# A gated FFN beside a long convolution on one core: the conv blocks' loads tied to slots by one-column writes, first kernel rows and FFN leftovers asked for at other places

## The chip, the core and the metric

The kernel runs on one core of a Trainium2 chip. The core has a matrix engine (PE, with its weight loads shown as PEld), a vector engine (DVE), a scalar engine (ACT), a general engine (POOL) and a queue engine (SP), which work side by side and wait for one another by semaphores. Matmul results land in PSUM banks; everything else lives in SBUF. DMA transfers are asked for by an instruction of SP, ACT or POOL, in the order of that engine's own instructions. The metric is the time of one execution in microseconds (us), as the median of several runs.

## What is computed

A layer norm of `x` (2048 positions, 512 channels) feeds two branches. One is a state-space convolution: a kernel `K` of 2048 taps for each channel, made of 128 complex modes, is convolved with the normalised input by FFT, and a skip term is added. The other is a two-layer FFN with a gelu between and a silu behind. The output is `x` plus their product. Cut from the reference:

```python
xn = _layernorm(x)
P = exp((dt * A)[:, :, None] * l)                 # A complex, 512 x 128
K = einsum("dn,dnl,dn->dl", Cc, P, dB).real       # 512 x 2048
s = irfft(rfft(pad(xn.T)) * rfft(pad(K)))[:, :L].T + xn * Dskip
g = silu(gelu(xn @ w1 + b1) @ w2 + b2)            # 512 -> 1792 -> 512
return x + s * g
```

## The kernel before, in words

The work has two parts that follow one another.

**FFN and generation of K.** The first part, up to about 394 us, is played from `ORDER` (line 48), a list of tokens written out by hand; each token calls one function of the table `acts` (line 733), and every engine executes its own instructions in the order in which they were written. The FFN works in 56 steps: four quarters of the positions, twice, with half of the hidden units each time. `F` are the matmuls of the first layer, `G` gelu, `H` and `R` the split of the result into a high and a low part, `S` the matmuls of the second layer (line 277, three matmuls a call, written as `z`). Beside them K is made in 32 pieces; `UD` (line 663) stores a piece from `ko` to the DRAM tensor `kgd`. `KL0` calls `kernel_load(0)`, which loads the first block's kernel rows from `kgd` into `in`; `SL1.g` calls `side_piece(1, g)`, which loads a quarter of block 1's input rows into `raw`. `ZD` stores a gated quarter of the FFN's output to `gd`.

**The last FFN steps.** From line 1071 on the rest is written as a small program. `S0` to `S3` and `L0` to `L3` are the second-layer matmuls of the last two FFN steps. `F00`, `F01`, `F10`, `F11` are the first DFT of conv block 0 (line 864, 64 matmuls of a 32 x 128 weight and 64 columns each; the first digit is 0 for the input and 1 for the kernel rows, the second is the half of the channels), each with its four copies out of PSUM (`first_out`, line 875, two on ACT and two on DVE). A first DFT takes four banks of PSUM. Each `L` is followed on DVE by `z_add`, which adds the first half's sums `zi` (1 MB, loaded by `z_load`, line 398); `A0` to `A3` are silu on ACT. Around these stand the loads of the tables `mc` (line 798, four pieces of 512 KB, the second DFT's cosines and sines) and of `tcn` (`ct_load`, line 806, four pieces of 512 KB, the back DFT's table). `mc_turn` (line 802) makes a negated copy `mn` of a piece on ACT.

**The conv blocks.** Four blocks of 128 channels follow, each of eight slots (`slot`, line 980). Slot `g` of block `b` holds on PE the second DFT of four frequencies (line 882, 64 matmuls, written as `s` like the first DFT), in some slots a back DFT (line 921, written as `sa`) of this block or the one before, in the even slots a first DFT of the next block, and in one slot the last DFT (line 961, written as `y`) of the block before. ACT copies out: `spectrum` (`uh`), the first DFT's outputs (`X`) and the back DFT's (`Z`). DVE multiplies (`product`), combines (`combine`), transposes (`turn`) and, after the last DFT, multiplies by the gate `gb` (`last_out`, line 969), whose sum with `xb` POOL forms. Stores of a finished block go out on SP.

Loads of the blocks, before the change:

- `side_piece` loads four quarters of the input rows of block `b + 2` in slots 3, 4 and 5 of block `b`. One quarter is 256 KB in 128-byte runs. In slot 7 ACT turns `raw` into `in` (`side_turn`, line 837).
- `kernel_load(b + 2)` loads two halves of 512 KB at slot 7; `kernel_load(1)` stands in slot 2 of block 0, on ACT's queue. `side_skip` (line 859) adds the skip coefficient to the rows on POOL.
- `tail_load(b - 1, t)` loads `gb` and `xb` of the block before, quarter by quarter (256 KB each), in slots 0 to 3; the last block's own (`last`) in slots 3 to 6 of the last block.
- `mc` pieces 2 and 3 and `tcn` pieces 1, 2 and 3 are loaded in block 0 on ACT's queue, `mc_turn` 2 and 3 stand in slots 1 and 3.

The tiles named `in` and `raw` share two buffers (tag `in`), so a tile of that tag waits until the readers of the one before the last are through. A load is asked for as soon as its queue has come to it and its tile is free.

Of the kernel before, what the change touches and what calls it, by code (L numbers as in the profile page):

```python
# [11 lines left out]
F32 = mybir.dt.float32  # L12
# [8 lines left out]
P = 128  # L21
L, D, NS, F = 2048, 512, 128, 1792
# [3 lines left out]
N1, N2 = 32, 64  # L26
NB = 4
DB = P // NB
# [4 lines left out]
NQ = L // P  # L33
TB = 4
NTB = NQ // TB
# [86 lines left out]
F.52.1 F.53.0 KL.31.1 UD.26 E.28.1 E.28.2 Z.30 B.30.0 F.53.1 C.30.0 R.51 E.29.0 S.49.2 E.29.1 A.30.1 G.52  # L122
S.49.3 UD.27 Q.28 B.30.1.1 C.30.1 ST S.50.0 SL1.2 H.52 E.29.2 N.30.0 S.50.1 S.50.2 U.28 A.31.0 S.50.3
G.53 S.51.0 F.54.0 B.31.0 C.31.0 A.31.1 Z.31 S.51.1 Q.29 S.51.2 F.54.1 R.52 B.31.1.1 F.55.0 C.31.1 S.51.3
N.30.1 S.52.0 N.31.0 F.55.1 E.30.0 U.29 N.31.1 E.30.1 ZG.2 E.30.2 E.31.0 S.52.1 Q.30 H.53 E.31.1 UD.28
UD.29 S.52.2 R.53 S.52.3 S.53.0 E.31.2 G.54 H.54 U.30 G.55 S.53.1 Q.31 ZD.2 UD.30 H.55 R.54 R.55 U.31
S.53.2 S.53.3 UD.31 KL0
"""


# [37 lines left out]
def kernel(  # L168
# [5 lines left out]
    V, A, GP, PE, SY = nc.vector, nc.scalar, nc.gpsimd, nc.tensor, nc.sync  # L174
# [118 lines left out]
    SB = {}  # L293
# [103 lines left out]

    def z_load(t):
        zi = wka.tile([P, NB, TB, P], F32, tag="zi", name=f"zi{t}")
        (A if t == NTB - 1 else SY).dma_start(zi, za[t])  # L400
        fin[t] = zi

    def bias_load():
# [378 lines left out]
    def open_front():  # L782
        SB["pf"] = pf = opened(p2, "pf", "right")
        SB["mc"] = pf.tile([P, N1, 2, N2], F32, name="mc")
        SB["mn"] = pf.tile([P, N1, N2], F32, name="mn")
        SB["psa"] = opened(p2, "psa", "right", bufs=2, space=PSUM)
# [8 lines left out]
        gx[0] = new_tail(0)  # L795
        yy[0, "T", 1] = new_turn(0, 1)

    def mc_load(j, q=SY):
        k, w = slice(8 * j, 8 * j + 8), 16 * N2
        q.dma_start(SB["mc"][:, k].rearrange("p k a m -> p (k a m)"), cm[:, w * j:w * j + w])  # L800

    def mc_turn(j):
        k = slice(8 * j, 8 * j + 8)
        A.mul(SB["mn"][:, k], SB["mc"][:, k, 1], -1.0)

    def ct_load(j, q=SY):
        k, w = slice(8 * j, 8 * j + 8), 8 * P
        q.dma_start(SB["tcn"][:, k].rearrange("p k m -> p (k m)"), ct[:, w * j:w * j + w])

    side, xf, fp = {}, {}, {}  # L810
    turns = [0]
# [13 lines left out]

    def side_piece(b, g):
        t = side.setdefault(b, SB.get("raw1"))
        SY.dma_start(t[g * N1:(g + 1) * N1], xs.rearrange("(n m) (b g d) -> b g n m d", n=N1, b=NB, g=G)[b, g])

    def side_load():  # L830
# [18 lines left out]
    def kernel_load(b):  # L849
        if b:  # L850
            k = SB["pf"].tile([P, DB, N2], F32, tag="in", name=f"in1_{b}", bufs=2)
            k = [k[:, :DB // 2], k[:, DB // 2:]]
        else:
            k = [wka.tile([P, DB // 2, N2], F32, tag="x", name=f"in1_0_{h}", bufs=2) for h in range(2)]
        for h in range(2):
            (A if b == 1 else SY).dma_start(k[h], kgd[b].rearrange("p (h d m) -> p h d m", h=2, m=N2)[:, h])
        side[b].append(k)

    def side_skip(b):
        for h in range(2):  # L860
            k0 = side[b][1][h][:, :, 0]
            GP.tensor_add(k0, k0, dsk[:, b, h * DB // 2:(h + 1) * DB // 2])  # L862
# [19 lines left out]
    def second_dft(b, g):  # L882
        mc, mn = SB["mc"], SB["mn"]
        p = SB["ps"].tile([P, 2, 2, 2, 2, N2], F32, tag="ri", name=f"s2_{b}_{g}", bufs=2)
        for jj in range(2):
            for o in range(2):
                for c in range(2):
                    for ka in range(2):
                        for r in range(2):
                            k, h = 4 * g + 2 * jj + ka, slice(r * 64, (r + 1) * 64)  # L890
                            w = mn[h, k] if o > c else mc[h, k, c != o]
                            PE.matmul(p[ka * 64:(ka + 1) * 64, r, o, :, jj], w,  # L892
                                      xf[b][h, c, :, k, :], start=(c == 0), stop=(c == 1), skip_group_check=True)
        sp[b, g] = p
# [55 lines left out]
    gx = {}  # L950

    def tail_load(b, t):
        if b not in gx:
            gx[b] = new_tail(b)
        for d, src in zip(gx[b], (gd[b][t], ux[b, t])):
            SY.dma_start(d[:, t * TB:(t + 1) * TB].rearrange("p q m -> p (q m)"), src)

    def new_tail(b):
        return tuple(SB["pm"].tile([P, NQ, P], F32, tag=m, name=f"{m}{b}") for m in ("gb", "xb"))
# [20 lines left out]
    def slot(b, g):  # L980
        nxt = b + 1 < NB
        last = not nxt
        i = g // 2
        sa = {3: (b, 0), 5: (b, 1), 7: (b, 2)}
        if b:
            sa[1] = b - 1, 3
        if b and nxt:
            sa[6] = sa.pop(5)
        sa = sa.get(g)
        end = b and g == 5 - last  # L990
        if b and nxt and g == 4:
            turn(b - 1, 1, 1)
        if last and g == 6:
            turn(b, 0, 0)
        second_dft(b, g)
        if sa:
            back_dft(*sa)
        if end:
            py = [bank(f"y{b - 1}_{n}").rearrange("p e m -> p (e m)") for n in range(G)]
            last_dft(b - 1, 0, py)  # L1000
            last_dft(b - 1, 1, py)
        if nxt and g % 2 == 0:
            first_dft(b + 1, i // 2, i % 2, range(G))
        turning = b + 2 < NB and g == 7
        if turning:
            side_turn(b + 2, (0,))
        spectrum(b, g)
        if turning:
            side_turn(b + 2, (1,))
        if sa:  # L1010
            back_out(*sa)
        if nxt and g % 2 == 0:
            first_out(b + 1, i // 2, i % 2, (A, A, V, V) if b and g == 4 else (A, A, A, A))
        product(b, g)
        if last and g > 5:
# [12 lines left out]
        if b and g == 2:  # L1028
            turn(b - 1, 1, 0)
        if last and g == 3:  # L1030
            turn(b - 1, 1, 1)
        if b and g < 4:
            tail_load(b - 1, g)
        if last and g == 3:
            big = SB["pf"].tile([P, 2, N1, P], F32, tag="X0", name="last")
            gx[b] = big[:, 0, :NQ], big[:, 1, :NQ]
        if last and 2 < g < 7:
            tail_load(b, g - 3)
        if b + 2 < NB and 2 < g < 6:
            if g == 3:  # L1040
                side[b + 2] = SB["pf"].tile([P, N2, DB], F32, tag="in", name=f"raw{b + 2}", bufs=2)
            for n in {3: (0,), 4: (1,), 5: (2, 3)}[g]:
                side_piece(b + 2, n)
        if b and g == 7 - last:
            for t in range(NTB):
                store(b - 1, t, SY)
        if b == 0 and g < 7:
            if g in (0, 2):
                mc_load(2 + g // 2, A)
            if g in (1, 3):  # L1050
                mc_turn(2 + g // 2)
                ct_load(1 + g // 2, A)
            if g == 2:
                kernel_load(1)
            if g == 3:
                side_skip(1)
            if g == 5:
                ct_load(3, A)
        if b + 2 < NB and g == 7:
            kernel_load(b + 2)  # L1060
        if 0 < b < NB - 1 and g == 1:
            side_skip(b + 1)

    with tc.manual_schedule():
        prologue()
# [5 lines left out]
    with tc.manual_schedule():  # L1071
        SB["spare"] = False
        open_front()
        for j in range(2):
            mc_load(j)
        side_skip(0)
# [27 lines left out]
        b = NB - 1  # L1104
# [65 lines left out]
```

## Time and profile before

| | us |
|---|---|
| median of the runs | 573.61 |
| lowest and highest of 3 runs | 572.51 and 575.36 |
| the profiled execution | 571.65 |
| span of the profiled execution, first to last instruction | 569.9 |
| mean granted clock of the matrix engine | 0.978 |

The profile is of one execution. Its span is 1.75 us shorter than that execution's time, and the execution lies a little below the runs' median. For each engine there is its busy time; a chain of waits follows the work back from the last instruction and says at each step what it waited for; timelines list the instructions of an engine in order of time (start, duration, engine, line, operation, `out<-in`, count, and in brackets the idle time before it and what ended it); stretches give busy time of each engine, the granted clock (PEclk, 1 is full), the share of DMA time and GB/s. "issue" is time in which an engine waited for nothing that the profile shows. In these views numbers behind `L` are lines of the kernel before.

### The profile page before, as it was taken

To read this page: it belongs to the slowest core of one execution; us is meant where nothing else is said; L and a number is where in the kernel's file an instruction comes from. 1 tells how busy PE (TensorE), PEld (TensorE's weight loads), DVE (VectorE), ACT (ScalarE), POOL (GpSimd) and SP (SyncE) were. 2 spreads that over 40 slices of the span, in tenths; PEclk is the share of its full clock that TensorE was granted. 3 is DMA by queue.
4 is the path that set the end of the run, shared out by engine and by line. 5 is a ranking of instruction groups with operands and counts; after the bars stand their busy time and mean duration, and the time that the engine had idled before them with its cause. 6 is when DMAs were issued, how large, how long until landed. Compare 5 with 4: busy or idle time off the path is not lost.

```text
span 569.9 us, 17562 instructions
## 1 busy us (share of the span) xinstructions
PE 541.0 (95%) x7511; PEld 432.5 (76%) x7511; DVE 448.2 (79%) x685; ACT 401.5 (70%) x580; POOL 279.0 (49%) x383
## 2 busy tenths in 40 slices
PE   8898999999999999999999999999897989999993
PEld 7666777777777777777777777777787878898972
DVE  6899989999899789998896867884243558466985
ACT  3687898899877998787998787895354743743320
POOL 5556388459874779969642872550210001103032
PEclk9998999999999999999999999999789999999998
DMA  8847335835291456570366029104539366432732
GB/s 229 294 152 236 134 129 162 254 124 204 57 368 39 117 167 187 201 193 22 105 198 180 20 99 187 43 26 152 204 125 216 79 229 67 171 131 76 258 117 76
DMA packets 88394, 85.88 MB, mean 151 GB/s; under 512 B 42262, under 2 KB 65050, under 8 KB 87292
## 3 DMA queue, kind: packets, MB, share of 16 engines
q1 hardware_dynamic: 78096, 61.68, 36.7%
q0 software_dynamic: 8768, 17.83, 10.2%
q10 hardware_dynamic: 1452, 5.25, 3.0%
q8 instruction: 59, 0.97, 0.7%
q14 instruction: 19, 0.16, 0.1%
HBM read 51.18 MB, written 33.55 MB: 149 GB/s over the span
## 4 chain that ended last, share of the span: by engine, by line
PE 72%; DVE 17%; DMA 4%; issue 3%; ACT 2%; POOL 1%; ACTq 0%; DVEq 0%; POOLq 0%
PE s L892 11%; PE z L287 8%; PE z L288 7%; PE z L289 7%; PE f L248 7%; PE f L250 6%; PE f L249 6%; PE sa L928 5%; PE s L872 5%; PE kg L655 5%; PE ph L591 2%; DMA zi<-za 2%; DVE hl L274 2%; DVE e L644 1%; DMA in<-kgd 1%
## 5 line engine op out<-in xcount | busy, mean ns | idle before, releaser
L617 POOL TENSOR_TENSOR mm<-mm,rc 128x32 f32<-128x32 f32 (+4 forms) x150 | 116.8, 779 | 11.8
L287 PE MATMUL z<-w2h,hh 128*128 128x512 f32 x224 | 99.4, 444 | 0.0
L248 PE MATMUL f<-xh,w1h 128*128 128x512 f32 x220 | 91.3, 415 | 0.0
L289 PE MATMUL z<-w2h,hl 128*128 128x512 f32 x224 | 89.7, 401 | 0.3 <-DVE hl L274 0.3
L288 PE MATMUL z<-w2l,hh 128*128 128x512 f32 x224 | 89.8, 401 | 0.0
L250 PE MATMUL f<-xh,w1l 128*128 128x512 f32 x220 | 87.1, 396 | 1.7 <-DVE w1l L233 1.7
L249 PE MATMUL f<-xl,w1h 128*128 128x512 f32 x220 | 86.7, 394 | 0.0
L909 DVE TENSOR_TENSOR t<-s,uh 128x512 f32<-128x512 f32 x64 | 41.0, 682 | 49.2 <-ACT uh L900 48.8
L892 PE MATMUL s<-X,mc 64*64 64x128 f32 x1536 | 63.3, 279 | 1.3 <-issue 1.3
L274 DVE TENSOR_TENSOR hl<-hf,hh 128x512 fp32r<-128x512 f32 x56 | 50.2, 899 | 5.2 <-ACT hh L268 5.2
L892 PEld LDWEIGHTS s<-X,mc 64*64 64x64 f32 x1536 | 47.6, 137 | 7.1 <-issue 3.1
L614 POOL COPY mm<-rc 128x32 f32<-128x32 f32 x30 | 12.9, 430 | 80.9 <-DVE e L647 56.3
L262 ACT ACTIVATE hf<-f,b1s 128x512 f32<-128x512 f32 x56 | 38.2, 687 | 20.2 <-DVE hl L274 10.1
L289 PEld LDWEIGHTS z<-w2h,hl 128*128 128x128 f32 x224 | 42.8, 191 | 11.0 <-DVE hl L274 0.7
L250 PEld LDWEIGHTS f<-xh,w1l 128*128 128x128 f32 x220 | 41.3, 188 | 12.8 <-DVE w1l L233 3.0
L287 PEld LDWEIGHTS z<-w2h,hh 128*128 128x128 f32 x224 | 43.1, 193 | 10.1 <-issue 0.6
L605 DVE SCALAR_TENSOR_TENSOR ra<-ra,ph 128x512 f32<-128x512 f32 x64 | 43.6, 681 | 8.8 <-ACT ra L599 7.7
L288 PEld LDWEIGHTS z<-w2l,hh 128*128 128x128 f32 x224 | 43.1, 192 | 8.5 <-DVE w2l L233 0.2
L248 PEld LDWEIGHTS f<-xh,w1h 128*128 128x128 f32 x220 | 41.5, 189 | 9.1
L249 PEld LDWEIGHTS f<-xl,w1h 128*128 128x128 f32 x220 | 41.4, 188 | 9.1
L640 DVE TENSOR_TENSOR e<-mm,ra 128x1024 f32<-128x1024 f32 x32 | 43.1, 1346 | 6.0 <-ACT ra L628 2.6
L872 PE MATMUL s<-fc,in 32*128 32x64 f32 x1024 | 40.4, 286 | 6.3 <-POOL in L862 3.0
(178 smaller groups left out, 1148.0 us busy)
## 6 DMA issues: line engine op xcount, KB each, us to landing
x<-in_A_u_dram SPq DMA_DIRECT2D x8, 512.0 KB
xs<-x SPq DMA_DIRECT2D x8, 512.0 KB
xt_h<-xh POOLq DMA_DIRECT2D x4, 1024.0 KB, 5.3
xt_l<-xl POOLq DMA_DIRECT2D x4, 1024.0 KB, 7.6
kgd<-ko SPq DMA_DIRECT2D x32, 128.0 KB
za<-zo SPq DMA_DIRECT2D x4, 1024.0 KB
xh<-xt_h POOLq DMA_DIRECT2D x4, 1024.0 KB, 6.1
xl<-xt_l POOLq DMA_DIRECT2D x4, 1024.0 KB, 9.8
```

The source lines that it names most:

```text
L248: PE.matmul(p, wh[:, k, :], xh[:, k, :], start=(k == 0), stop=False)
L249: PE.matmul(p, wh[:, k, :], xl[:, k, :], start=False, stop=False)
L250: PE.matmul(p, wl[:, k, :], xh[:, k, :], start=False, stop=(k == KD - 1))
L274: V.tensor_sub(hl, hf, hh)
L287: PE.matmul(z, hh[:, s], wh, start=(f0 == 0 and not rows), stop=False)
L288: PE.matmul(z, hh[:, s], wl, start=False, stop=False)
L289: PE.matmul(z, hl[:, s], wh, start=False, stop=(f0 == FA - 1))
L605: V.scalar_tensor_tensor(ra[:, 0, c], ra[:, 1, c], MAGIC, p, op0=ALU.subtract, op1=ALU.subtract)
L617: GP.tensor_mul(mv[:, :, 0:3:2, w:2 * w], mv[:, :, 0:3:2, 0:w], rc[:, 2 + 2 * i:4 + 2 * i, :].rearrange("p j c -> p c j").unsqueeze(3).to_ ...
L640: V.tensor_mul(e1, m1.unsqueeze(1).to_broadcast([P, 2, CH, N1]), ra[:, :, :, :N1])
L872: PE.matmul(p[:, i, :], src[r, 2 * i:2 * i + 2, :], fc[r], start=True, stop=True, skip_group_check=True)
L892: PE.matmul(p[ka * 64:(ka + 1) * 64, r, o, :, jj], w, xf[b][h, c, :, k, :], start=(c == 0), stop=(c == 1), skip_group_check=True)
```

## The change

Four things change.

- **Column writes.** A new function `pace(t)` writes zeros to one column of a tile with DVE. It is called ahead of a load for `mc` pieces 2 and 3, `tcn` pieces 1 to 3, the kernel rows of blocks 1 to 3 (each half), the raw quarters of blocks 2 and 3 and `gb` of every tail quarter. The load overwrites that column, so it waits for the write, and the write waits for DVE to come to it.
- **Slots.** The raw quarters come one at the start of slot 3 and one each at the ends of slots 3, 4 and 5. The kernel rows of blocks 2 and 3 come half by half in slots 0 and 1 of the block before, with `side_skip` in slot 3. The tails come in slots 0, 1 and 2 (two quarters in the last), in the last block two each in slots 0 and 1, and the last block's own in slots 2 to 5. `tcn` pieces come in slots 1, 3 and 6, `mc` pieces still in slots 0 and 2, the `mn` turns in slots 2 and 4.
- **Queues.** The loads of `mc`, `tcn`, `zi` and the kernel rows of block 1 that ACT asked for are asked for by SP.
- **Places.** `KL0` moves forward in `ORDER`, ahead of the stores `UD.28` to `UD.31`. The last `zi` load moves ahead of the first `mc` load. `kernel_load(1)` and `mc_turn(0)` move behind `F10` and its outputs, `mc_turn(1)` behind `F11`'s.

```diff
-S.53.2 S.53.3 UD.31 KL0
+S.53.2 S.53.3 UD.31
...
-N.30.1 S.52.0 N.31.0 F.55.1 E.30.0 U.29 N.31.1 E.30.1 ZG.2 E.30.2 E.31.0 S.52.1 Q.30 H.53 E.31.1 UD.28
+N.30.1 S.52.0 N.31.0 F.55.1 E.30.0 U.29 N.31.1 E.30.1 ZG.2 KL0 E.30.2 E.31.0 S.52.1 Q.30 H.53 E.31.1 UD.28
...
     def z_load(t):
-        (A if t == NTB - 1 else SY).dma_start(zi, za[t])
+        SY.dma_start(zi, za[t])
...
+    def pace(t):
+        V.memset(t, 0.0)
+
-    def mc_load(j, q=SY):
+    def mc_load(j):
+        if j > 1:
+            pace(SB["mc"][:, 8 * j, 0, :1])
-    def ct_load(j, q=SY):
+    def ct_load(j):
+        if j:
+            pace(SB["tcn"][:, 8 * j, :1])
...
     def side_piece(b, g):
+        if b > 1:
+            pace(t[g * N1:(g + 1) * N1, 0, :1])
...
     def kernel_load(b):
-        for h in range(2):
-            (A if b == 1 else SY).dma_start(k[h], kgd[b].rearrange("p (h d m) -> p h d m", h=2, m=N2)[:, h])
         side[b].append(k)
+        for h in range(2 if b < 2 else 0):
+            kernel_half(b, h)
+
+    def kernel_half(b, h):
+        k = side[b][1][h]
+        if b:
+            pace(k[:, 0, :1])
+        SY.dma_start(k, kgd[b].rearrange("p (h d m) -> p h d m", h=2, m=N2)[:, h])
...
     def tail_load(b, t):
+        pace(gx[b][0][:, t * TB, :1])
...
         second_dft(b, g)
+        if b + 2 < NB and g == 3:
+            side[b + 2] = SB["pf"].tile([P, N2, DB], F32, tag="in", name=f"raw{b + 2}", bufs=2)
+            side_piece(b + 2, 0)
...
-        if b and g < 4:
-            tail_load(b - 1, g)
-        if last and g == 3:
-            big = SB["pf"].tile([P, 2, N1, P], F32, tag="X0", name="last")
-            gx[b] = big[:, 0, :NQ], big[:, 1, :NQ]
-        if last and 2 < g < 7:
-            tail_load(b, g - 3)
+        if b and nxt:
+            if g == 0:
+                kernel_load(b + 1)
+            if g < 2:
+                kernel_half(b + 1, g)
+        if nxt and g == 3:
+            side_skip(b + 1)
+        if b and g < (3 if nxt else 2):
+            for t in range(NTB)[(slice(0, 1), slice(1, 2), slice(2, 4))[g] if nxt else slice(2 * g, 2 * g + 2)]:
+                tail_load(b - 1, t)
+        if last and 1 < g < 6:
+            if g == 2:
+                big = SB["pf"].tile([P, 2, N1, P], F32, tag="X0", name="last")
+                gx[b] = big[:, 0, :NQ], big[:, 1, :NQ]
+            tail_load(b, g - 2)
+        if b == 0:
+            if g in (0, 2):
+                mc_load(2 + g // 2)
+            if g in (2, 4):
+                mc_turn(1 + g // 2)
+            if g in (1, 3, 6):
+                ct_load((1 + g) // 2)
         if b + 2 < NB and 2 < g < 6:
-            for n in {3: (0,), 4: (1,), 5: (2, 3)}[g]:
-                side_piece(b + 2, n)
+            side_piece(b + 2, g - 2)
...
-        if b == 0 and g < 7:
-            if g in (0, 2):
-                mc_load(2 + g // 2, A)
-            if g in (1, 3):
-                mc_turn(2 + g // 2)
-                ct_load(1 + g // 2, A)
-            if g == 2:
-                kernel_load(1)
-            if g == 3:
-                side_skip(1)
-            if g == 5:
-                ct_load(3, A)
-        if b + 2 < NB and g == 7:
-            kernel_load(b + 2)
-        if 0 < b < NB - 1 and g == 1:
-            side_skip(b + 1)
...
         open_front()
+        z_load(NTB - 1)
         for j in range(2):
             mc_load(j)
...
                 first_out(0, *k, (A, A, V, V))
-                if k == (0, 0):
-                    z_load(NTB - 1)
-                    mc_turn(0)
-                if k == (1, 0):
-                    mc_turn(1)
+                if k[0]:
+                    mc_turn(k[1])
+                    if k[1] == 0:
+                        kernel_load(1)
```

More of the change, by code (lines that the diff above doesn't have):

```diff
@@ L796, in open_mid @@
         yy[0, "T", 1] = new_turn(0, 1)
-    def mc_load(j, q=SY):
+    def pace(t):
+        V.memset(t, 0.0)
+    def mc_load(j):
         k, w = slice(8 * j, 8 * j + 8), 16 * N2
-        q.dma_start(SB["mc"][:, k].rearrange("p k a m -> p (k a m)"), cm[:, w * j:w * j + w])
+        if j > 1:
+            pace(SB["mc"][:, 8 * j, 0, :1])
+        SY.dma_start(SB["mc"][:, k].rearrange("p k a m -> p (k a m)"), cm[:, w * j:w * j + w])
     def mc_turn(j):
@@ L804, in mc_turn @@
         A.mul(SB["mn"][:, k], SB["mc"][:, k, 1], -1.0)
-    def ct_load(j, q=SY):
+    def ct_load(j):
         k, w = slice(8 * j, 8 * j + 8), 8 * P
-        q.dma_start(SB["tcn"][:, k].rearrange("p k m -> p (k m)"), ct[:, w * j:w * j + w])
+        if j:
+            pace(SB["tcn"][:, 8 * j, :1])
+        SY.dma_start(SB["tcn"][:, k].rearrange("p k m -> p (k m)"), ct[:, w * j:w * j + w])
     side, xf, fp = {}, {}, {}
@@ L1031, in slot @@
             turn(b - 1, 1, 1)
-        if b and g < 4:
-            tail_load(b - 1, g)
-        if last and g == 3:
-            big = SB["pf"].tile([P, 2, N1, P], F32, tag="X0", name="last")
-            gx[b] = big[:, 0, :NQ], big[:, 1, :NQ]
-        if last and 2 < g < 7:
-            tail_load(b, g - 3)
+        if b and nxt:
[20 more added lines that the diff above has]
+                ct_load((1 + g) // 2)
         if b + 2 < NB and 2 < g < 6:
-            if g == 3:
-                side[b + 2] = SB["pf"].tile([P, N2, DB], F32, tag="in", name=f"raw{b + 2}", bufs=2)
-            for n in {3: (0,), 4: (1,), 5: (2, 3)}[g]:
-                side_piece(b + 2, n)
+            side_piece(b + 2, g - 2)
         if b and g == 7 - last:
@@ L1046, in slot @@
                 store(b - 1, t, SY)
-        if b == 0 and g < 7:
-            if g in (0, 2):
-                mc_load(2 + g // 2, A)
-            if g in (1, 3):
-                mc_turn(2 + g // 2)
-                ct_load(1 + g // 2, A)
-            if g == 2:
-                kernel_load(1)
-            if g == 3:
-                side_skip(1)
-            if g == 5:
-                ct_load(3, A)
-        if b + 2 < NB and g == 7:
-            kernel_load(b + 2)
-        if 0 < b < NB - 1 and g == 1:
-            side_skip(b + 1)
     with tc.manual_schedule():
```

## The prediction

> **What bounds the kernel now.** I read the engines' totals first, then the chain of waits around the end of the FFN, then the timelines of PE, ACT, DVE and SP there.
>
> ```profile
> PE 541.0 (95%) x7511; PEld 432.5 (76%) x7511; DVE 448.2 (79%) x685; ACT 401.5 (70%) x580; POOL 279.0 (49%) x383
> ```
>
> PE is busy for 95% of the span, so a change of transfers can win only what PE idles or runs slowly. The chain of waits from the last FFN steps through the conv's block 0 (start, us, what) shows both.
>
> ```profile
> 397.36 10.19 DMA zi<-za
> ...
> 407.77 0.69 DVE zi L429
> ...
> 409.11 4.27 PE s L872 x60
> ...
> 416.24 3.06 PE s L892 x64
> 419.30 1.94 PE s L872 x64
> ...
> 428.36 7.95 DMA in<-kgd
> ...
> 438.67 3.24 PE s L892 x64
> ...
> 449.71 0.86 issue
> ...
> 451.11 1.99 PE sa L928 x32
> 453.10 1.91 PE s L892 x64
> ```
>
> Two transfers stand on the chain: zi (1 MB), asked for at 397.36 and waited for by DVE until 407.77, and the kernel rows of block 1 (in<-kgd), asked for at 428.36. Around them the same 64 matmuls take longer: s at L892 3.06 and 3.24 us against 1.91, s at L872 4.27 (60 of 64) against 1.94. The stretches of time say why (PE, PEld, DVE, ACT and POOL busy, then PEclk, DMA share, GB/s).
>
> ```profile
> 402.00:404.00 2.00, 0.97 (x12) 0.53 (x13) 0.13 (x1) 1.59 (x3) 2.00 (x2) 1.00 1.02 416
> 404.00:406.00 2.00, 2.00 (x59) 2.00 (x58) 0.00 (x0) 0.00 (x0) 0.44 (x1) 0.73 0.99 412
> ...
> 434.00:436.00 2.00, 0.00 (x0) 0.00 (x0) 0.00 (x0) 1.06 (x2) 0.00 (x0) 1.00 1.14 283
> ...
> 440.00:442.00 2.00, 2.00 (x38) 1.67 (x31) 0.00 (x0) 0.74 (x3) 0.00 (x0) 0.50 1.16 155
> ```
>
> The granted clock falls after each idle stretch: within 404 to 406, and to 0.50 by 440. So a stall costs twice, its own length and the slow stretch behind it. The reader should also see DMA at a share of 1 until 406: zi shares the way with what SP had issued just before.
>
> ```profile
> 390.15 4.32 SPq L665 DMA_DIRECT2D kgd<-ko  x2
> 394.51 1.19 SPq L856 DMA_DIRECT2D in<-kgd  x2
> ```
>
> **The front, moved parts.** KL0 (1 MB of in<-kgd) goes forward on SP, to right behind the raw piece SL1.2, at about 368; nothing of it is left at 394.5. The zi load goes from ACT to SP, to right behind the last kernel-row store, so it issues at 394.5 at the head of the queue, with mc behind it. It lands between 397.1 (2.6 us, 1 MB at the 412 GB/s above) and 402.5 (7.95 us, what in<-kgd took on a shared way); its first reader, DVE's z_add(0), follows L0's matmuls, which end at 402.3 (next fence). The mn turns move behind the outputs of F10 and F11, and with them goes ACT's wait for mc.
>
> ```profile
> 402.12 0.63 ACT L804 ACTIVATE mn<-mc 128x512 f32<-128x512 f32 x1 [3.95 <-DMA mc<-in_cm_dram]
> ...
> 397.27 1.29 DVE L878 COPY X<-s 128x512 f32<-128x512 f32 x2 [5.18 <-PE s L872]
> ...
> 397.13 0.50 PE L287 MATMUL z<-w2h,hh 128*128 128x512 f32 x1
> ...
> 398.72 2.01 PE L872 MATMUL s<-fc,in 32*128 32x64 f32 x64
> 400.67 0.50 PE L287 MATMUL z<-w2h,hh 128*128 128x512 f32 x1
> ...
> 403.33 3.11 PE L872 MATMUL s<-fc,in 32*128 32x64 f32 x64 [0.99 <-POOL in L847]
> ```
>
> The idle of 0.99 before F10 (403.33) is put down to POOL, but F10's banks came free only when ACT had copied F01 out, behind the mn turn. What is late next: each first DFT needs the four banks of the one before, and DVE's copies end 1.43 us after it (397.13 to 398.56). Six z matmuls take 1.59 us (397.13 to 398.72) and cover that; three take 0.80 and don't. So F10 runs from 400.67 + 1.59 = 402.26 to 404.20; its outputs end at 405.63, which leaves 0.65 us of idle behind L1; F11 ends at 407.6, L2 and L3 at 409.25, and slot 0 starts there instead of at 416.24: **7.0 us**. ACT fits: F10's outputs, one mn turn (0.63), a table load and a silu, then F11's outputs by about 409.
>
> **Half clock at the new idle.** First DFTs seem to count little for the clock. It fell when 1 us of idle stood beside F10, and stayed up after a longer gap between sa matmuls:
>
> ```profile
> 462.41 0.94 PE L928 MATMUL sa<-tcn,Y 64*128 64x128 f32 x11 [1.71 <-issue]
> ```
>
> F10, L1, 0.65 us of idle and F11 look like the pattern that brought it down. Bounds: 0, and at half clock from F11 through slot 0: 2.3 (4.27 - 1.94) + 1.3 (L2 and L3, from 409.11 + 4.27 = 413.38 to 416.24, so 2.86 - 1.59) + 1.15 (3.06 - 1.91) = 4.8. No row lies between, so I take about the middle: **-2.5**.
>
> By the Trainium skill (TensorE: Matmul & The Clock Gate, Part 1: The HAM clock gate) the clock halves after an idle window of about 3.4 us, and the window runs free. By that rule nothing in the changed front would bring it down. The trace disagrees on the length, since less than 1 us of idle sufficed; what the rule would make of the time is rival A.
>
> **Block 0.** kernel_load(1) now stands behind F10, its halves held by a column write each: issue at about 405.7 instead of 428.36. At 7.95 us it is there by 414, and its first reader is slot 4's first DFT, at 409.25 + 5 x 1.91 + 2 x 1.94 + 1.99 = 424.7. The loads of mc and ct leave ACT's queue for SP's.
>
> ```profile
> 436.66 2.01 PE L872 MATMUL s<-fc,in 32*128 32x64 f32 x64 [2.95 <-POOL in L862]
> ```
>
> Block 0 at full clock is 8 x 1.91 + 4 x 1.94 + 3 x 1.99 = 29.0 us; it takes 453.10 - 416.24 = 36.86. The 7.9 between are idle 2.95, half clock 2.8 (1.15 and 1.33 in s, 0.3 in sa), issue 1.5 (0.86 in the chain above and 0.6 of the list below) and small gaps. I leave 1.3 of issue and gaps: **6.6 us**.
>
> **Held loads.** 35 column writes on DVE: mc 2, ct 3, in<-kgd 6, raw 8, gb and last 16. The nearest row is a memset of the same shape.
>
> ```profile
> L191 DVE MEMSET eps<- 128x1 f32 x1 | 0.1, 59 | 0.8 <-PEq L1155 0.8
> ```
>
> 35 x 0.059 = 2.1 us, mostly inside DVE's waits for uh; in block 3, where DVE hardly waits, 8 x 0.059 = 0.5. Bounds 0 and 2.1; I take **-0.3**. Behind a write DVE holds the next slot's products, and ACT and PE behind them; but the tiles written over were last read a slot or more before (raw: by the first DFT of slot 2, which ends as DVE gets there), so I count no wait. On SP every later transfer stands behind a held one. The tight ones are the fourth raw piece, released at the end of slot 5 (in block 1 behind last_out) and due at ACT's turn in slot 7, and the tail of block 2, due at last_out in block 3.
>
> ```profile
> 367.82 0.60 SPq L828 DMA_DIRECT2D raw<-xs  x1
> ...
> 371.00:371.50 0.50, 0.50 (x4) 0.43 (x4) 0.50 (x1) 0.50 (x2) 0.50 (x1) 1.00 0.01 1
> ...
> 444.55 0.69 DVE L917 TENSOR_TENSOR Y<-t,t 128x512 f32<-128x512 f32 x1
> ...
> 449.96 1.99 ACT L847 COPY in<-raw 128x1024 f32<-128x1024 f32 x1
> ...
> 480.82 2.48 DVE L974 TENSOR_TENSOR gb<-y,gb 128x512 f32<-128x512 f32 x4
> ...
> 488.89 2.02 ACT L847 COPY in<-raw 128x1024 f32<-128x1024 f32 x1
> ...
> 458.00:460.00 2.00, 2.00 (x62) 1.83 (x56) 0.56 (x1) 1.84 (x4) 0.38 (x2) 1.00 1.01 385
> 534.67 0.69 DVE L917 TENSOR_TENSOR Y<-t,t 128x512 f32<-128x512 f32 x1
> ...
> 543.59 2.48 DVE L974 TENSOR_TENSOR gb<-y,gb 128x512 f32<-128x512 f32 x4 [0.27 <-issue]
> ```
>
> A lone piece is through 3.2 us after its issue (367.82 to 371.0). In block 0 the fourth is released at 445.2 and due at 449.96, in block 1 at 483.3 and 488.89: 1.5 and 2.4 us to spare. The second half of block 2's tail is released at 535.4; 1 MB at 385 GB/s is 2.7 us, with as much again for latency and for the first half ahead of it 540.8, due at 543.59. All hidden. With the cover gone, each microsecond late is one of ACT or DVE, and soon of PE.
>
> The first DFT after a block's end waits for ACT's Z copies, which stand behind the raw turn:
>
> ```profile
> 493.86 2.48 PE L872 MATMUL s<-fc,in 32*128 32x64 f32 x60 [0.54 <-ACT Z L939]
> ```
>
> That is 0.54 + 2.48 - 1.94 = 1.0 us in block 1's case. In block 0 the gap at 449.71 let ACT catch up; I charge **-0.5**. PE's issue gaps in the conv are these:
>
> ```profile
> PE s L892 <- issue: 2.2, 2, 1.3
> PE sa L928 <- issue: 1.7, 1, 1.7
> PE s L872 <- issue: 0.9, 2, 0.6
> ```
>
> 4.8 in all, 1.5 of it counted in block 0. DMA ran full near the longest (458 to 460). Thinner bursts may shorten the other 3.3; bounds 3.3 and, if a burst meets a fetch, -2; I take **0.8**.
>
> Sum: 7.0 - 2.5 + 6.6 - 0.3 - 0.5 + 0.8 = 11.1. The profiled execution took 571.65 (span 569.9 and 1.75 around it), which gives 560.6; the median of the runs shown, 573.61, gives 562.5. I state 561.5.
>
> **Rivals.** (A) *No half clock*: 2.5 more, and with the issue gaps mostly gone about 1.5 on top, 557.5. For it: the clock is down nowhere in blocks 1 to 3, gaps and all. Against: F10, a short z and idle are what stood before the fall at 404. (B) *Half clock lasts*: down at F11's start and on through slots 0 and 1: 2.3 + 1.3 + 1.15 + 2.3 + 1.15 = 8.2 instead of 2.5, so 567.2. For it: before it lasted from 405 through the s at 416.24. Against: that one s ended it. (C) *Held transfers land late*, which ends slower: loads are released so near their use that the turn or last_out waits. It acts in five places (raw turn in blocks 0 and 1, last_out in blocks 1 to 3), with 1.5 to 3 us to spare in each; to turn a gain of 11 into a loss of 3 each must come 3 us late, so land 4.5 to 6 us later than worked out. That gives 576.5 and more. For it: four raw pieces in a row kept SP for long.
>
> ```profile
> 428.01 15.89 SPq L828 DMA_DIRECT2D raw<-xs  x4
> ```
>
> Against: those stood beside five other loads; now they come one a slot. The Trainium skill (DMA: Bandwidth & Descriptors, Rules for kernel authors) speaks for this rival: issue a DMA early and wait for it late. The trace agrees at 397.36 and 428.36, and says nothing on loads issued just early enough. (D) *The holds hold nothing*, since SP waits for the tiles' readers anyway: then only the front and block 0 count, and the 0.8 goes; that is within the forecast.
>
> **How the numbers follow.** Forecast with D (558.5 to 565.5) 0.47; A (below) 0.20; B, or one load still waited for (565.5 to 570.7) 0.22; within 0.5% of the median, 2.9 us, about what a measurement of this kernel can tell from no change (570.7 to 576.5) 0.05; C above that 0.06. So faster 0.89. The range goes from 556 (A with the bounds of the issue gaps) to 569.5 (B and a load 2 us late) and leaves out 0.2.
>
> **What would show it.** Right: neither zi nor in<-kgd on the chain; slot 0 within 17 us of the last kernel-row store; s at L892 1.91 throughout block 0; the clock below 1 at most once. Wrong: DVE waiting at a column write, ACT waiting for DMA before the raw turn, DVE for gb before L974, a slow clock that reaches slot 1, or new issue gaps behind the released bursts.

## The result, and the profile after

| | before | after |
|---|---|---|
| median of the runs (4 of each, us) | 573.06 | 559.13 |
| lowest and highest (us) | 571.08 and 575.36 | 558.28 and 560.08 |
| the profiled execution (us) | 571.65 | 559.32 |
| its span (us) | 569.9 | 557.5 |
| its mean granted clock | 0.978 | 0.989 |

The ratio is 0.9756, with a 95% interval from 0.9715 to 0.9797: faster by 14 us. The changed kernel sent once more beside other kernels (e0 below) gave 0.9822 [0.9787, 0.9857], 10 us. The sum of the prediction, 11.1 us, lies between the two; the time that it stated was 561.5 us.

The totals of the engines, after:

```profile
PE 534.6 (96%) x7511; PEld 427.4 (77%) x7511; DVE 454.1 (81%) x720; ACT 401.0 (72%) x580; POOL 279.8 (50%) x383
```

The chain of waits of the changed kernel from the last kernel-row matmuls on, with the starts of the blocks (start, us, what). `L887` is the first DFT and `L907` the second, as `L872` and `L892` were before.

```profile
391.71 1.03 PE kg L655 x64
...
401.41 1.94 PE s L887 x64
...
404.26 2.53 PE s L887 x64
...
408.39 1.91 PE s L907 x64
...
415.89 1.92 PE s L887 x58
417.82 0.52 issue
418.33 0.44 PE s L887 x4
418.78 3.54 PE s L907 x64
422.31 1.99 PE sa L943 x32
...
439.79 0.71 PE s L907 x21
440.50 1.90 ACT in L856
442.40 0.98 ACT Z L954 x2
...
478.41 1.95 PE s L907 x64
...
516.26 3.65 PE s L907 x128
```

No transfer stands on it up to there; one is named later, in block 3 (see the holds below). From the last kg to slot 0 it is now 408.39 - 391.71 = 16.68 us. The same view of the kernel before, at the places that the prediction did not show (the last kg, and the starts of blocks 2 and 3):

```profile
392.64 1.03 PE kg L655 x64
...
491.05 1.95 PE s L892 x64
...
527.78 3.65 PE s L892 x128
```

| stretch | before | after | gained |
|---|---|---|---|
| last kg to slot 0 | 416.24 - 392.64 = 23.60 | 16.68 | 6.92 |
| block 0 | 453.10 - 416.24 = 36.86 | 439.79 - 408.39 = 31.40 | 5.46 |
| block 1 | 491.05 - 453.10 = 37.95 | 478.41 - 439.79 = 38.62 | -0.67 |
| block 2 | 527.78 - 491.05 = 36.73 | 516.26 - 478.41 = 37.85 | -1.12 |
| block 3 and the end | 569.9 - 527.78 = 42.12 | 557.5 - 516.26 = 41.24 | 0.88 |

That is 11.47; the rest of the 12.4 between the two spans (0.93) arose before the last kg, which starts anywhere from 390.35 to 393.05 in the profiles below. SP's timeline after shows the moved requests:

```profile
390.49 0.33 SPq L400 DMA_DIRECT2D zi<-za  x1
393.20 0.32 SPq L665 DMA_DIRECT2D kgd<-ko  x1
...
404.84 0.80 SPq L872 DMA_DIRECT2D in<-kgd  x2
```

zi is asked for ahead of the last kernel-row store, 6.9 us earlier than before and 4 us earlier than I had said. The stretches of time (PE, PEld, DVE, ACT and POOL busy, then PEclk, DMA share, GB/s) show the way empty before anyone needs zi (DVE's first z_add starts at 401.44), the clock up in the front, and where it is down now:

```profile
400.00:402.00 2.00, 2.00 (x30) 1.45 (x29) 1.75 (x3) 0.90 (x2) 0.00 (x0) 1.00 0.00 0
...
404.00:406.00 2.00, 2.00 (x52) 1.80 (x50) 1.36 (x5) 1.98 (x3) 0.00 (x0) 1.00 0.09 20
...
418.00:420.00 2.00, 1.67 (x34) 1.59 (x37) 0.72 (x4) 1.75 (x4) 0.00 (x0) 0.71 0.75 190
420.00:422.00 2.00, 2.00 (x44) 1.91 (x36) 0.00 (x0) 0.78 (x2) 0.00 (x0) 0.50 0.79 258
...
482.00:484.00 2.00, 2.00 (x66) 1.93 (x66) 2.00 (x4) 0.61 (x2) 0.00 (x0) 0.93 0.00 0
484.00:486.00 2.00, 2.00 (x45) 2.00 (x41) 0.91 (x3) 1.59 (x4) 0.00 (x0) 0.50 0.07 18
```

Each of the 35 column writes took 59 ns, and one of them waited, for 0.3 us. The group with that wait in the view by line (count, busy us and mean ns of one, idle before and what ended it):

```profile
L799 DVE MEMSET raw<- 32x1 f32 x8 | 0.5, 59 | 0.6 <-PE s L887 0.3
```

### The profile page after: what moved, and what is told of

The parts are those of the page before. It is cut to its first block, busy times and chain, and to the rows that moved or that the text cites. A ratio compares the mean times of both kernels' runs of the same rounds, so it can differ in the third digit from the quotient of the medians.

```text
span 557.5 us, 17629 instructions
## 1 busy us (share of the span) xinstructions
PE 534.6 (96%) x7511; PEld 427.4 (77%) x7511; DVE 454.1 (81%) x720; ACT 401.0 (72%) x580; POOL 279.8 (50%) x383
## 4 chain that ended last, share of the span: by engine, by line
PE 72%; DVE 19%; issue 3%; ACT 2%; DMA 1%; POOL 1%; DVEq 0%; ACTq 0%; SPq 0%; POOLq 0%
PE s L907 10%; PE z L287 8%; PE z L288 7%; PE z L289 7%; PE f L248 7%; PE f L250 7%; PE f L249 7%; PE s L887 6%; PE sa L943 5%; PE kg L655 5%; PE ph L591 2%; DVE hl L274 2%; DVE ra L605 2%; DVE e L644 2%; DVE e L640 1%
## 5 line engine op out<-in xcount | busy, mean ns | idle before, releaser
L617 POOL TENSOR_TENSOR mm<-mm,rc 128x32 f32<-128x32 f32 (+4 forms) x150 | 115.0, 766 | 11.8
L287 PE MATMUL z<-w2h,hh 128*128 128x512 f32 x224 | 97.8, 437 | 0.0
L289 PE MATMUL z<-w2h,hl 128*128 128x512 f32 x224 | 88.5, 395 | 0.3 <-DVE hl L274 0.3
L288 PE MATMUL z<-w2l,hh 128*128 128x512 f32 x224 | 88.6, 396 | 0.0
L907 PE MATMUL s<-X,mc 64*64 64x128 f32 x1536 | 63.7, 282 | 0.1
L274 DVE TENSOR_TENSOR hl<-hf,hh 128x512 fp32r<-128x512 f32 x56 | 53.2, 954 | 4.4 <-ACT hh L268 4.4
L907 PEld LDWEIGHTS s<-X,mc 64*64 64x64 f32 x1536 | 47.8, 138 | 5.5 <-DVE t L924 1.7
L893 ACT COPY X<-s 128x512 f32<-128x512 f32 x52 | 27.1, 597 | 25.0 <-PE s L887 25.0
```

The costliest lines, as they stand in the source:

```text
L274: V.tensor_sub(hl, hf, hh)
L287: PE.matmul(z, hh[:, s], wh, start=(f0 == 0 and not rows), stop=False)
L288: PE.matmul(z, hh[:, s], wl, start=False, stop=False)
L289: PE.matmul(z, hl[:, s], wh, start=False, stop=(f0 == FA - 1))
L617: GP.tensor_mul(mv[:, :, 0:3:2, w:2 * w], mv[:, :, 0:3:2, 0:w], rc[:, 2 + 2 * i:4 + 2 * i, :].rearrange("p j c -> p c j").unsqueeze(3).to_ ...
L907: PE.matmul(p[ka * 64:(ka + 1) * 64, r, o, :, jj], w, xf[b][h, c, :, k, :], start=(c == 0), stop=(c == 1), skip_group_check=True)
```

## The experiments

Theory: the places earn it all, since zi, the first kernel rows and block 1's kernel rows come in time and the clock then stays up. First rival: the holds earn it, by spreading the transfers. Second rival, for the front: one of the places would have done by itself. Ratios are to the kernel before on the same chip, with their 95% intervals.

### Places or holds

**e1, no holds.** The changed kernel; every load is asked for as soon as its queue and tile allow.

```diff
 def pace(t):
-    V.memset(t, 0.0)
+    pass
```

> The changed kernel with every column write left out; places, slots and queues stay. Theory P (the places at the front earn the gain, the holds are worth within 1.5 us): 558 to 561 against 559.1, with slot 0 again about 16.7 us behind the last ko matmuls. Rival H (holding the loads back earns a good part): 562 or more, with longer issue gaps of PE in blocks 1 to 3 than the changed kernel's 1.3 us.

560.73 us, ratio 0.9811 [0.9772, 0.985].

**e2, places alone.** The kernel before with KL0 forward, zi on SP ahead of `mc`, the mn turns behind F10 and F11 and `kernel_load(1)` behind F10, on ACT's queue. No holds, no other slots.

```diff
-S.53.2 S.53.3 UD.31 KL0
+S.53.2 S.53.3 UD.31
...
+        z_load(NTB - 1)
...
+                if k[0]:
+                    mc_turn(k[1])
+                    if k[1] == 0:
+                        kernel_load(1)
```

> The kernel before with only the places moved: KL0 forward, zi on SP ahead of mc, the mn turns behind F10 and F11, kernel_load(1) behind F10 (still asked for by ACT); the conv's slots and queues as before, no column writes. P: 559 to 561.5, so 12 to 14 us of the 13.9. H: 563 to 567.

559.31 us, ratio 0.9789 [0.9754, 0.9823].

**e3, holds alone.** The changed kernel with those places put back; the holds, the slots and the queues of the block loads stay.

```diff
...
-S.53.2 S.53.3 UD.31
+S.53.2 S.53.3 UD.31 KL0
...
-        SY.dma_start(zi, za[t])
+        (A if t == NTB - 1 else SY).dma_start(zi, za[t])
...
+        if b == 0 and g == 2:
+            kernel_load(1)
...
-        z_load(NTB - 1)
...
-                if k[0]:
-                    mc_turn(k[1])
-                    if k[1] == 0:
-                        kernel_load(1)
+                if k == (0, 0):
+                    z_load(NTB - 1)
+                    mc_turn(0)
+                if k == (1, 0):
+                    mc_turn(1)
```

> The changed kernel with the four places put back: KL0 last, zi on ACT behind F00, the mn turns behind F00 and F10, kernel_load(1) in slot 2 of block 0 (held, on SP). P: 570 to 574, with PE waiting for the kernel rows in slot 4 and half clock at the front. H: 565 to 569.

570.6 us, ratio 0.9983 [0.9949, 1.0017].

**e0, the changed kernel again**, as a control beside the kernels below.

> The changed kernel as it is, on the chip of the next ones: 557.5 to 560, the same as places alone gave within 2 us, if P holds; 3 us or more below that if the holds are worth something.

559.53 us, ratio 0.9822 [0.9787, 0.9857]. So the places earn the gain; the holds and the new slots earn nothing that these runs can tell, and show no cost: with places e0, e1 and e2 lie within 0.9789 to 0.9822, without them e3's interval holds 1. The intervals leave room for some 3 us either way.

### Block 1's kernel rows

**e10, `kernel_load(1)` alone.** The kernel before with one line moved.

```diff
                 if k == (1, 0):
                     mc_turn(1)
+                    kernel_load(1)
...
-            if g == 2:
-                kernel_load(1)
```

> The kernel before with nothing but kernel_load(1) moved behind F10 (still on ACT's queue, no column write). Theory: block 0's idle of 2.95 and the half clock behind it go, the front stays: 5 to 7 us below the kernel before. Rival: the rows, asked for at about 405 beside zi, mc and tcn, only delay zi, and the half clock of the front goes on into block 0: within 2 us of the kernel before.

566.31 us, ratio 0.9926 [0.9899, 0.9954]: some 4 us. In its profile block 0 takes 446.97 - 413.85 = 33.12 us, 3.7 less than before. Its front is about as slow as before, 413.85 - 390.70 = 23.15 us from the last kg to slot 0.

**e6, the reverse.** The changed kernel with `kernel_load(1)` back in slot 2, held, on SP.

```diff
+        if b == 0 and g == 2:
+            kernel_load(1)
...
-                    if k[1] == 0:
-                        kernel_load(1)
```

> The changed kernel with kernel_load(1) put back to slot 2 of block 0, held there by its column writes, on SP. Theory: the rows are asked for about 10.4 us behind slot 0 and due 17.9 us behind it; at 7.95 us to landing they are late by about half a us, and if they still share with raw as before by 3, with half clock behind: 560.5 to 564 against 559. Rival: on SP, ahead of the raw quarters, they land in 4 us and the place is worth nothing: the same as the changed kernel within 1 us.

562.04 us, ratio 0.9873 [0.9837, 0.9909]. That is 2.5 us above e0, and the two intervals just overlap. In its profile the rows are not late: SP's and POOL's timelines of e6 show them asked for at 418.89 and the skip added to the second half, the later one, at 426.66,

```profile
418.89 0.80 SPq L872 DMA_DIRECT2D in<-kgd  x2
...
426.66 0.23 POOL L877 TENSOR_TENSOR in<-in,dsk 128x16 f32<-128x16 f32 x1 [1.19 <-DMA in<-kgd]
```

and slot 4's first DFT starts at 427.83 without a wait. In the kernel before the same rows, asked for at 428.36 on ACT's queue, took 7.95 us, about as long. So what cost the time there was the late request; the slot itself would just do. What the 2.5 us of e6 are stays open: no wait for the rows shows, and the 1.9 us between the profiled executions of e6 and e0 are about one more spell of half clock (419.83 to 425.33 took 5.50 us for s and sa that take 3.90 at full clock).

### The front: which move earns it

All of these have `kernel_load(1)` behind F10, so their ratios compare with e10's.

**e9, only the mn turns moved beside it.** The changed kernel with KL0 back at the end and zi back on ACT behind F00.

```diff
-        z_load(NTB - 1)
...
+                if k == (0, 0):
+                    z_load(NTB - 1)
...
-        SY.dma_start(zi, za[t])
+        (A if t == NTB - 1 else SY).dma_start(zi, za[t])
...
-S.53.2 S.53.3 UD.31
+S.53.2 S.53.3 UD.31 KL0
...
```

> The changed kernel with KL0 put back to the end of ORDER and zi put back to ACT behind F00; the mn turns and kernel_load(1) stay moved. Theory (zi lands late because 3.5 MB share the way): DVE waits for zi until 405 to 407, slot 0 comes 4 to 6 us later, 563 to 566. Rival (the 0.99 us stall of F10 behind the mn turn, and the half clock it set off, were the cost of the front): 558.5 to 561.

566.17 us, ratio 0.9925 [0.9895, 0.9955], no better than e10. The chain of waits of e9, then PE's timeline there:

```profile
395.90 9.65 DMA zi<-za
...
407.71 3.60 PE s L887 x58
...
414.17 2.14 PE s L907 x64
```

```profile
407.11 0.43 PE L887 MATMUL s<-fc,in 32*128 32x64 f32 x2 [2.72 <-DVE X L893]
```

The wait before F10 is gone, as ACT no longer stands at the table, and zi, still late, makes F11 wait 2.72 us: DVE's copies of F10 stand behind the z_add that waits for zi.

**e13, only zi moved beside it.** The kernel before with two lines moved: `kernel_load(1)` as in e10, and zi on SP ahead of `mc`.

```diff
...
         open_front()
+        z_load(NTB - 1)
...
                 if k == (0, 0):
-                    z_load(NTB - 1)
                     mc_turn(0)
                 if k == (1, 0):
                     mc_turn(1)
+                    kernel_load(1)
```

> The kernel before with two lines moved: zi asked for on SP ahead of the mirror tables, and block 1's kernel rows asked for on ACT's queue behind F10. No holds, the kernel rows of slot 0 where they were, the mn turns where they were. Places theory, with either of the two early loads enough for the front: 558.5 to 561 us, a ratio of 0.978 to 0.982, the same as the whole change; kg's end to slot 0's product 16.7 to 17.7 us. Rival (the holds or the mn turns earn a part when the kernel rows come late): 562 to 566 us.

566.73 us, ratio 0.9921 [0.9893, 0.9949], again no better than e10; I had expected the whole gain. Eleven of its twelve executions took 565.16 to 571.75 us at a mean clock of 0.972 to 0.983, one took 561.26 at 0.992. Its profile is of the longest of them and serves here for the order of events alone. Timelines of e13, first ACT's, then DVE's and PE's:

```profile
403.40 0.63 ACT L804 ACTIVATE mn<-mc 128x512 f32<-128x512 f32 x1 [5.18 <-DMA mc<-in_cm_dram]
403.94 1.05 ACT L878 COPY X<-s 128x512 f32<-128x512 f32 x2
...
402.42 0.69 DVE L429 TENSOR_TENSOR zi<-z,zi 128x512 f32<-128x512 f32 x1 [0.24 <-PE z L289]
...
404.60 3.70 PE L872 MATMUL s<-fc,in 32*128 32x64 f32 x58 [2.22 <-POOL in L847]
```

zi is in time: DVE's z_add waits for PE's z, not for the transfer. But `mc` now stands behind zi on SP and lands 1.3 us later than before (the mn turn starts at 403.40, in the kernel before at 402.12). ACT waits 5.18 us for it with F01's copies queued behind, and F10 waits 2.22 us for the banks. The profile names POOL as the releaser. The times name ACT: its two copies take 1.05 us from 403.94, so the first ends near 404.5, and F10 starts at 404.60. The clock then falls and stays down until slot 0, as in the kernel before; stretches of e13:

```profile
404.00:406.00 2.00, 1.40 (x22) 1.43 (x22) 0.00 (x0) 0.99 (x3) 1.73 (x1) 0.66 0.19 62
...
416.00:418.00 2.00, 2.00 (x26) 1.35 (x29) 0.93 (x2) 1.08 (x2) 0.00 (x0) 0.50 0.00 0
```

**e5, both.** The changed kernel with KL0 back at the end of `ORDER`; zi first and the mn turns moved.

```diff
...
-S.53.2 S.53.3 UD.31
+S.53.2 S.53.3 UD.31 KL0
```

> The changed kernel with the kernel rows of slot 0 alone put back to the end of the phase; zi stays on SP ahead of the mirror tables. Either-is-enough theory: with zi at the head of SP's queue the 1 MB lands before F11 even with the kernel rows behind it, and the kernel rows, 1 MB asked for some 8 us before slot 0's product, land in time too: kg's end to slot 0 stays at 16.7 to 17.7 us, 559 to 561 us. Rival (both are needed, because the two transfers share the way): 3 to 6 us of the 6.6 come back, 562.5 to 565.5 us, with F11 or slot 0's product late behind a DMA.

559.06 us, ratio 0.9795 [0.9757, 0.9833]: the whole gain. **e8, mn turns and KL0.** The changed kernel with zi back on ACT behind F00, as the first three pieces of e9's edit.

> The changed kernel with zi alone put back to ACT's queue behind F00; the kernel rows stay early. Either-is-enough theory: zi has the way nearly to itself and lands late by 1 us at most: 559.5 to 561 us. Rival (zi's own place is what earned the front): issued some 4 to 5 us later, with the mirror tables now ahead of it, it comes 5 to 7 us late and the stall in F11 returns: 564.5 to 566.5 us.

561.8 us, ratio 0.9822 [0.9782, 0.9862]: the same as e0. The last kg and slot 0 in the chains of waits, first of e5, then of e8:

```profile
390.86 1.03 PE kg L655 x64
...
407.53 1.91 PE s L907 x64
```

```profile
391.86 1.03 PE kg L655 x64
...
408.66 1.91 PE s L907 x64
```

Beside `kernel_load(1)` behind F10:

| mn turns moved | zi first on SP | KL0 forward | last kg to slot 0 (us) | ratio to before |
|---|---|---|---|---|
| no | no | no (e10) | 23.15 | 0.9926 [0.9899, 0.9954] |
| yes | no | no (e9) | 414.17 - 391.17 = 23.00 | 0.9925 [0.9895, 0.9955] |
| no | yes | no (e13) | 416.78 - 392.69 = 24.09, in its longest execution | 0.9921 [0.9893, 0.9949] |
| yes | yes | no (e5) | 16.67 | 0.9795 [0.9757, 0.9833] |
| yes | no | yes (e8) | 16.80 | 0.9822 [0.9782, 0.9862] |
| yes | yes | yes (e0) | 408.64 - 391.96 = 16.68 | 0.9822 [0.9787, 0.9857] |

Two waits stand one behind the other in the front: ACT's for `mc`, which holds F10's banks, and DVE's for zi, which holds F11's. Taking one away earns nothing, taking both earns some 6 to 7 us. Most of that is the slow clock: in each profile whose front is left with a wait it goes to half, for 6.84 us in e3 and e9, 10.24 in e10 and 13.7 in e13 and in the kernel before, and in the nine whose front has neither it stays up. In e9 the idle of 2.72 and half of the 6.84 us make 6.1 of the 6.3 us that its front is longer than the changed kernel's (an estimate, from s, which takes 3.53 us instead of 1.91 at half clock). For zi either of two moves is enough: asked for first, or with 1 MB of kernel rows out of its way. (e9, e5, e8 and e0 have the holds and e10 and e13 have not; by e0 to e3 that makes no difference. The mn turns left in place with KL0 forward was not tried.)

### The waits and the clock in the blocks

**e4, half a turn later.** In the changed kernel the second half of the raw turn moves behind ACT's Z copies, for which PE waits at the first DFT of the next block's slot 0.

```diff
-        if turning:
-            side_turn(b + 2, (1,))
...
+        if turning:
+            side_turn(b + 2, (1,))
```

> The changed kernel with the second half of ACT's raw turn in slot 7 put behind the copies Z of the back DFT. If the first DFT of the next block waits for Z behind the turn, the 0.88 and 0.54 us of PE idle and the slow 60 matmuls behind them go: 556.5 to 557.5 against 559.1, and less half clock behind them. Rival: ACT's copies uh of the next slot are what counts, which come later by the same work: 558.5 to 559.5.

559.28 us, ratio 0.9784 [0.9748, 0.9819]: not to be told from the changed kernel. PE's waits in e4 from 404 to 545 (total us, times, longest):

```profile
PE s L907 <- issue: 4.1, 4, 1.9
PE s L887 <- issue: 1.4, 2, 1.1
```

The waits of the first DFTs for Z are gone, but there are 5.5 us of issue gaps, at other matmuls; the changed kernel's own profile has 1.8.

**e12, no idle ahead of a first DFT.** The changed kernel with six more matmuls by the identity (recorded as twelve), ahead of the first of the four first DFTs of blocks 2 and 3 (in slot 0 of blocks 1 and 2), into the bank that it overwrites (added work).

```diff
+        for n in range(6 if b > 1 and u + h == 0 else 0):
+            PE.matmul(ps[0][:, 0], ident, ident, start=True, stop=True, skip_group_check=True)
```

> The changed kernel with six more matmuls by the identity on TensorE ahead of the first DFT of blocks 2 and 3, into the bank that this DFT then overwrites (work beside the computation; the outputs are the reference's). Idle theory (the spells of half clock in the first DFTs are set off by TensorE's idle time just before them): no spell at the start of blocks 2 and 3, the first DFT's 64 matmuls of block 2 at 1.9 to 2.0 us where the changed kernel's execution has 3.57, 557.5 to 559.5 us. Rival (the spells come wherever they fall): spells as often, 559 to 561 us, the six matmuls costing under 0.5 us each time.

560.14 us, ratio 0.981 [0.9758, 0.9862]: no gain. PE's timeline of e12 around the filled DFT of block 3 (slot 0 of block 2), then the chain of waits at two that were not filled:

```profile
484.64 1.60 PE L885 MATMUL s<-ident 128*128 128x128 f32 x12
486.17 2.01 PE L890 MATMUL s<-fc,in 32*128 32x64 f32 x64
```

```profile
474.17 1.08 ACT Z L957 x2
...
477.29 3.27 PE s L910 x64
...
512.06 1.08 ACT Z L957 x2
...
515.18 3.57 PE s L910 x64
```

Behind the filled DFTs the clock stayed up, but it fell behind two others that by the chain stood behind ACT's Z (their 64 matmuls took 3.02 us instead of 2.01, from 474.27 and 512.16), and beside issue gaps of 1.75 and 1.56 us at 419.6 and 464.0: four spells instead of two. Filling one place does not keep the clock up.

## Why the prediction was right, and where it was not

**Front, 7.0 predicted, 6.92 measured.** Right in size and in its steps: F10 starts 401.41 - 391.71 = 9.70 us after the last kg (worked out: 402.26 - 392.64 = 9.62), slot 0 16.68 us after it (worked out: 16.6). F11's 64 matmuls took 2.53 instead of 1.94, which is the 0.65 us of idle behind L1. That POOL was not F10's releaser, but ACT behind the mn turn, is borne out by e13 (and by e10, where ACT's first copy of 400.76 ends near 401.3 and F10 starts at 401.43). Two things failed without harm: zi was asked for at 390.49 and not at 394.5, for the load stands ahead of the last kernel-row store on SP; and the one term of 7.0 for three moves did not say that KL0 and zi replace each other, and that zi's move does nothing unless the mn turns move too.

**Half clock, -2.5 in the front.** This term was wrong: half clock did not come there in the changed kernel's two profiles (after F11 the s at 408.39 takes 1.91), nor in the seven others whose front has neither wait (e1, e2, e4, e5, e6, e8, e12). F10, L1, 0.65 us of idle and F11 were not enough. It came in the blocks instead: 422.31 - 418.78 = 3.53 for slot 3's s, and in block 2

```profile
481.71 1.99 PE s L887 x58
483.70 3.57 PE s L907 x64
```

or 1.62 + 1.66 = 3.3 us. So the sum came out by luck: a cost expected in one place fell in others. Two of the signs that the prediction named for being right failed with it, s at 1.91 throughout block 0 and the clock below 1 at most once. Rival A (no half clock, 557.5) had the front right and the blocks wrong; rival B (through slot 1) did not happen. The Trainium skill (TensorE: Matmul & The Clock Gate, Part 1: The HAM clock gate) ties half clock to an idle window of about 3.4 us. By these runs the spells in the blocks are that long (3.42 us), but idle of 0.5 to 1.3 us beside a first DFT was enough ahead of those of the changed kernel's two profiles, and the same idle often did nothing; more on this in the last section.

**Block 0, 6.6 predicted, 5.46 measured.** in<-kgd is asked for at 404.84 (worked out: 405.7) and nothing waits for it, as predicted. The difference is the spell at 418.78 (1.62); the issue gap there was 0.52 where 1.3 was left for gaps.

**F(2,0,0) behind the raw turn, -0.5 predicted.** Mis-sized: from the start of block 1 the chain goes over ACT's turn and Z (1.90 and 0.98 at 440.50), and PE waits for Z at the first DFTs in blocks 1 and 2:

```profile
PE s L887 <- ACT Z L954: 1.4, 2, 0.9
PE s L907 <- issue: 1.3, 2, 1.1
PE s L887 <- issue: 0.5, 1, 0.5
```

1.4 against 0.5 in the kernel before. Taking it away (e4) earned nothing measurable.

**Issue gaps, 0.8 predicted.** They fell from 4.8 to 0.5 + 1.3 = 1.8, in block 0 from 1.5 to 0.5 and behind it from 3.3 to 1.3. But e4 has 5.5 us with all the holds, so one profile of each can't credit it to them, and e1 without holds has 2.6 and is no slower. What sets their length is open; one of them stands at the same matmul, after 58 of 64 of F(1,0,1), in both profiles of the changed kernel (0.52 and 1.08 us) and in all others but e1's (0.25 to 1.75).

**Holds, -0.3 predicted.** No cost that shows: no DVE wait at a column write but 0.3 (0.9 in e0 and e4; the prediction counted none), no ACT wait for a raw quarter. The chain names one held transfer, in block 3:

```profile
527.05 3.52 DMA last<-gd
```

But DVE, which it is said to release, worked from 524.53 to 534.50 without a wait that the profile lists, and the PE wait behind it is 0.2 us; the last DFT there needs the transpose that DVE ended at the same time. So this is not a wait for the load. Rival C (held transfers late) failed; the fourth raw quarter of block 2 is asked for at 434.01, and ACT turns it at 438.03 with no wait for a transfer. Rival D (the holds hold nothing) names the outcome in time, though by another reason than it gave: the loads do move, and nothing on the path feels it. The Trainium skill (DMA: Bandwidth & Descriptors, Rules for kernel authors) says to issue a DMA early, and the runs agree at the moved places; for loads that were early enough, early or just in time made no difference that shows (e1 and e0).

## What to carry to other kernels

Where two waits stand one behind the other on different engines, each move alone measures as nothing; test them in pairs before calling one useless. Follow a PE wait through the in-order queue of the engine that frees its banks (here ACT, blocked by a table that no one needed yet), and don't take the named releaser on trust when the times don't meet. Loads that are early enough gain nothing by being held to a schedule; spend the effort on the few that are late, and first look at what shares their way.

## What was not expected of the hardware

**Half clock comes in steps of 3.41 us on a fixed grid.** Stretches of 1 us put the edges of the spells to a few hundredths of a us. After, the clock is half for 3.42 us from 418.84 and again from 483.70, and the two starts lie 64.86 us apart, 19 x 3.41. The four spells of e12 start at 419.62, 464.00, 477.64 and 515.20, which is 13, 17 and 28 steps of 3.41 behind the first. In the front it lasts for several steps: before, four (13.66 us from 404.92), and the next spell, from 439.06, starts ten steps behind the first. In the blocks each spell costs some 1.6 us. From slot 0's first DFT to 545 us the changed kernel's profiles have two (after) and one (e0), e4's none and e12's four. That is enough to spread executions of one kernel: of e12's six, those at a mean clock of 0.992 took 558.5 to 558.8 us, those at 0.981 and 0.982 took 565.1 and 566.3.

**First DFTs count little for the clock, as the prediction guessed.** Each profile with a spell (13 of the 14) can be laid out in stretches on its own grid, and PE's time in first DFTs taken off. From 393 to 530 us the clock fell behind 31 full-clock steps. In 27 of them PE was busy for at most 0.6 us with anything but a first DFT; among the 424 behind which it did not fall there is one such step. The other four had 0.82 to 1.39 us (the fall in the front of the kernel before came behind 0.83). From half clock it rose behind every step with 2.2 us or more of other matmuls and behind none with 1.8 or less. So what mostly goes before a fall is a first DFT and some idle that fall into one step with little else, and where the grid lies decides whether they do. This is a pattern in the traces; no run set out to test it.

**Two DVE subtractions slow down beside a POOL copy.** After, POOL's turn of block 1's rows comes earlier and stands beside two of DVE's `hl` subtractions, each of 0.69 us before:

```profile
388.12 4.51 POOL L856 COPY in<-raw 128x1024 f32<-128x1024 f32 x2 [8.70 <-ACT hf L262]
...
388.76 4.43 DVE L274 TENSOR_TENSOR hl<-hf,hh 128x512 fp32r<-128x512 f32 x2 [0.76 <-ACT hh L268]
```

The two took 4.43 us together, and the copy 4.51. PE lost 0.2 us by it. In e5 the copy comes later and takes 3.95 (400.68); a z_add beside it (403.82), one of whose inputs lies in PSUM, takes its usual 0.69. The Trainium skill (GPSIMD Engine Reference, 8. Key points) says that POOL shares its SBUF interfaces with DVE and that DVE's instructions with two SBUF inputs contend; the traces agree.
